# Attention's v loaded whole, its raw weight pieces in two buffers, w_in by wider pieces: one kernel of attention, experts and a second layer

## The chip, the cores and the metric

One NeuronCore of a Trainium2 chip runs the whole program. The metric is the device time of one execution in microseconds (us); less is better. A profiled execution gives the span (from the first to the last instruction) and the trace from which the rows below are taken.

## The reference

Three layers follow each other on 4608 tokens of width 512. First an attention within chunks of 64 tokens, for 8 heads of 64 features:

```python
scores = scale * np.matmul(q_c, k_c.transpose(0, 1, 2, 4, 3))
scores = scores - np.max(scores, axis=-1, keepdims=True)
attn = np.exp(scores)
attn = attn / (np.sum(attn, axis=-1, keepdims=True) + 1e-09)
out = np.matmul(attn, v_c)
```

Then a layer of 8 experts (512 to 1024 to 512 with a relu between), of which each token goes to the one with the highest gate logit and is weighted by its softmax. Last a second layer over all tokens, with float64 weights `w_in` (512 x 2048) and `w_out` (2048 x 512):

```python
h = x @ w_in
g = np.maximum(h, 0.0) + alpha * np.minimum(h, 0.0)
return (g @ w_out).astype(np.float32)
```

## The kernel before, in words

The tokens are 36 tiles of 128. The attention works on one tile (two chunks) in a step; the order of all parts of a step, and how many steps back each of them works, is a table written by hand (`STEP`), walked by the loop at the end of `attention_and_routing`. A part's instructions go to their engines' queues in this order, and each queue runs in order. In a step TensorE computes the scores of the next tile (`scores`, L651), turns the exponents (`transpose_p`, L671), multiplies them by v (`weigh`, L688, into the accumulator `av`), and turns the result (`transpose_x`, L714); every second step it computes gate logits (`logits`, L734) and turns them (`turn_logits`, L750). DVE takes the maxima (`peak`, L656), divides by the sums of the rows (`normalise`, L700 to L703) and adds the logits (`sum_logits`, L756). ACT does the exponentials (L664) and copies (L676, L721). Later steps also rank the tokens of each expert and build a table of places (`rank` L799, `spot_low` L840, `spot_high` L847, `place` L857).

q, k and v come in pairs of tiles, all on SP's queue: q whole, on 128 partitions; k and v by halves. Two heads lie on the partitions. For k and v each half of the partitions is written into columns of its own and the rest is zero (`kbd`, `vbd`, zeroed once by memsets), so a product over all 128 partitions serves two heads at once. Two such operands exist of each, used in turns; a load waits on SP until the operand's last use is over, and what stands behind it on SP waits too.

Beside the attention the kernel converts the float64 weights of the second layer (`Float64Weights`). There are 32 pieces: piece 2f is 128 columns of `w_in`, piece 2f + 1 is 128 rows of `w_out`. A piece is loaded raw (512 KB), and passes the stages `bits` (DVE, L227 and L228), `round` (ACT L238, POOL L239), `square` (ACT L245), `mask` (DVE, L253) and `finish` (ACT L266, POOL L267). In the attention a piece takes three steps (table `CONV`): `bits` and `round` in the first, `square` and `mask` in the second, `finish` in the third. `bits` reads and `mask` last reads the raw buffer. With one buffer the next load is issued after `mask`:

```python
conv.use(cpool, 1)
```

Twelve pieces are converted in the attention. The other twenty follow in the first of the second layer's 12 groups, where two raw buffers exist. Before step f of that group, `experts_and_ffn` makes sure that enough pieces are finished; its tables hold enough conversions that this loop adds none.

After the attention a tail, again in an order by hand (`TAIL`), ends the routing while the first blocks of one expert are computed. Then the second layer and the experts run side by side, also by tables, mostly bound to TensorE.

Of the kernel before, what the change touches and what calls it, by code (L numbers as in the profile page):

```python
# [20 lines left out]
N = 4608            # tokens  # L21
D = 512             # model width
H = 8               # heads
E = 8               # experts
F = 1024            # expert width
F2 = 2048           # second layer's width
NF = F2 // P
NT = N // P         # token tiles
NPAIR = NT // 2
KMAX = NT           # blocks of 128 tokens of one expert: at most this many  # L30
NCODE = E * KMAX
MID = float(N // 2)
HP = H // 2         # pairs of heads
ROW = D + 4         # a row of the expert layer's output, and its token's row
GT = 3              # token tiles in a group of the second layer
NG = NT // GT
GW = GT * P
ROUTE = (12, 8, 4, 4, 4, 4)  # token tiles that are ranked together
EARLY = 3           # after these, some expert surely has GT full blocks: its first GT blocks come first
assert sum(ROUTE) == NT and ROUTE[-1] == 4 and sum(ROUTE[:EARLY]) * P >= E * GW  # L40
ENDS = {sum(ROUTE[:i + 1]): n for i, n in enumerate(ROUTE)}
TE = sum(ROUTE[:EARLY])  # rows of x_tok, g_tok and out: by place in the tile, then tile, first TE tiles, then the others
V65 = 64 + 1         # columns of a head of v: its features and a one
RAWS = 2            # pieces of expert weights being loaded

# The other tokens: slots of up to two blocks of one expert, first the pairs of full blocks, then pairs with a second
# block that is not full, then single blocks. With NP slots for pairs, at most E single blocks are left.
# [4 lines left out]
FP, FS = F // P, F // PAIR  # steps of a pair's slot, of a single block's  # L52

# A step of the attention: its parts in order, each for the tile so many steps back.
# [12 lines left out]
# A step of the second layer, and with it one of the experts: in the first group, with single blocks, and the others.  # L67
# [32 lines left out]
FRONT = 30           # steps of the experts in the first group  # L100
# [24 lines left out]
# Before the first step of the second layer.  # L125
# [7 lines left out]
HOLD = 5            # steps of the second layer that are finished tile by tile  # L133

def surely_done(n):
    """Tokens in the first n slots, and before them: at least this many."""
# [18 lines left out]
class Float64Weights:  # L155
    """The second layer's float64 weights, rounded to float32 from their words, in two parts of 12 bits each.

    Piece 2 * f is columns f * 128 to f * 128 + 127 of w_in, piece 2 * f + 1 is rows f * 128 to f * 128 + 127 of w_out.
    """

    PIECES = 2 * NF
    # The square of the smallest high word (read as float32) whose number is a normal float32.
# [10 lines left out]
    def hold(self, pool):  # L173
        """Room for half of the parts."""
        f = NF // 2
        self.parts.append([
            pool.tile([P, 4, f * P] if i < 2 else [P, f, D], F32R, name=f"w{i}_{len(self.parts)}") for i in range(4)
        ])
# [4 lines left out]

    def w_out_part(self, part, f):
        return self.parts[f // (NF // 2)][2 + part][:, f % (NF // 2), :]

    def use(self, pool, bufs):
        """The pool for the pieces from here on."""
        assert self.piece is None and self.masked is None
        self.pool, self.bufs, self.ahead = pool, bufs, 1  # L190
        self.load()

    def leave(self):
        """The pieces loaded are the last of this pool."""
        self.ahead = 0

    def load(self):
        i, f = self.loaded, self.loaded // 2
# [4 lines left out]
        if i % 2 == 0:  # L203
            src = self.w_in.rearrange("(c p) f -> p c f", p=P)[:, :, f * 2 * P:(f + 1) * 2 * P]
            self.nc.sync.dma_start(raw.rearrange("p (c f) -> p c f", c=4), src)
        else:
            self.nc.sync.dma_start(raw, self.w_out[f * P:(f + 1) * P, :])
        self.raws[i] = raw

    def tick(self):  # L210
        """The next stage of a piece."""
# [6 lines left out]
    def bits(self):  # L218
        """The next piece: sign, exponent (its bias 127 for 1023) and the mantissa's bits in the high word."""
# [13 lines left out]
    def round(self):  # L233
        """The low word, rounded to 2^29."""
# [12 lines left out]
    def mask(self):  # L247
        """Zero for what is too small for a normal float32."""
# [7 lines left out]
    def finish(self):  # L256
        if self.masked is None:
            return
        nc, i, f, wf = self.nc, self.finished, self.finished // 2, self.masked
        self.finished, self.masked = i + 1, None  # L260
        if i % 2 == 0:
            hi, lo = self.w_in_part(0, f), self.w_in_part(1, f)
            wf = wf.rearrange("p (c f) -> p c f", c=4)
        else:
            hi, lo = self.w_out_part(0, f), self.w_out_part(1, f)
# [4 lines left out]
class Group:  # L270
    """Two layers over a few token tiles: activations by feature, then by token, every operand in two parts."""
# [11 lines left out]
    def take(self, rows, i, bank):  # L283
        """Token tile i of the group: its columns to partitions."""
# [29 lines left out]
    def up(self, key, wh, wl):  # L314
        """128 hidden features of all tokens."""
# [13 lines left out]
    def up_by_token(self, key, wh, wl):  # L329
        """The first tile's tokens, as many hidden features as the group is wide."""  # L330
# [27 lines left out]
    def down(self, acc, key, wh, wl, first, last, tiles=None):  # L358
        """Of some tiles: the last ones are the last that need this key."""
# [24 lines left out]
class Stream:  # L384
    """An expert's weights in pieces, in the order of their use: 256 columns of w1, then 256 rows of w2; each in two
    parts of 12 bits."""
# [8 lines left out]
    def add(self, index):  # L395
        """Another slot: where its expert's number is."""
        self.experts.append(index)
# [47 lines left out]
    def release(self, n):  # L445
        """Piece n has been used."""
# [20 lines left out]
class Gather:  # L467
    """The rows of a slot's tokens, their weights, and where they are."""
# [77 lines left out]
class Shared:  # L546
    """What the two parts of the kernel share."""


def attention_and_routing(ctx, tc, s_, qh, kh, vh, w_gate):  # L550
# [15 lines left out]
    # Operands with two heads on the partitions, each head's in its own columns, zeros elsewhere.  # L566
    kbd = [two.tile([P, 2, HP, 2 * P], F32, name=f"kbd{i}", bufs=1) for i in range(2)]
    vbd = [two.tile([P, 2, HP, 4, V65], F32, name=f"vbd{i}", bufs=1) for i in range(2)]
    for i in range(2):
# [3 lines left out]
        eng.memset(vbd[i][0:64, 1], 0.0)  # L573
        eng.memset(vbd[i][64:128, 0], 0.0)
# [6 lines left out]
    q_t = {}  # L581

    def load_halves(src, dst, j):
        for h2 in range(2):
            half = slice(h2 * 64, h2 * 64 + 64)
            d = dst[j % 2][half, h2]
            pat = "p a b -> p (a b)" if len(d.shape) == 3 else "p a b c -> p (a b c)"
            nc.sync.dma_start(d.rearrange(pat), src[j, half, :])
# [8 lines left out]
    def load_v(j):  # L597
        if j < NPAIR:
            load_halves(vh, vbd, j)
# [9 lines left out]
    # Constants.  # L609
# [72 lines left out]
    def weigh(t):  # L682
        a, vt = pt.pop(t), vbd[(t // 2) % 2]
        av = ps_av.tile([P, 2, 512], F32, tag="av", name="av")
        for hp in range(HP):
            for c in range(2):
                o = (hp % 2) * 2 * V65
                nc.tensor.matmul(  # L688
                    av[c * 64:c * 64 + 64, hp // 2, o:o + 2 * V65],
                    a[:, hp, c * 64:c * 64 + 64],  # L690
                    vt[:, :, hp, (t % 2) * 2 + c, :],
# [4 lines left out]
    def normalise(t):  # L696
# [7 lines left out]
            x.rearrange("p (a b d) -> p a b d", a=2, d=64), av[:, :, :, 0:64],  # L704
# [22 lines left out]
    def logits(t):  # L727
        """By pair of heads, each pair's on partitions of its own."""
# [33 lines left out]
    def choose(t0, n):  # L762
# [12 lines left out]
        # The gate's weight of the chosen expert: exp(0) over the sum.  # L775
# [608 lines left out]
```

## Time and profile before

| | |
|---|---|
| device time, three runs | 1571.5, 1567.76, 1571.31 us; median 1571.31 |
| span of the profiled execution | 1565.5 us, 24290 instructions |
| busy in it | PE 1492.6, DVE 841.7, ACT 662.9, POOL 454.1 us |
| DMA | 201.17 MB in 123508 packets |
| attention | first scores at 7.4 us, last at 163.0 us |
| second layer and experts | from about 236 us on |

The profiled execution's own time is not among the three runs; its span is the measure that belongs to the rows, and it lies 5.8 us below their median. PE is TensorE's matmuls, PEld its weight loads, SPq the issue of DMAs on SyncE's queue. In a row of instructions stand the start in us from the span's start, the duration, engine, line, operation, what is written from what, shapes and count, and in brackets how long the engine had stood idle and what ended that. A float32 product appears as two records.

### The profile page before, as it was taken

To read this page: it belongs to the slowest core of one execution; us is meant where nothing else is said; L and a number is where in the kernel's file an instruction comes from. 1 tells how busy PE (TensorE), PEld (TensorE's weight loads), DVE (VectorE), ACT (ScalarE), POOL (GpSimd) and SP (SyncE) were. 2 spreads that over 40 slices of the span, in tenths; PEclk is the share of its full clock that TensorE was granted. 3 is DMA by queue.
4 is the path that set the end of the run, shared out by engine and by line. 5 is a ranking of instruction groups with operands and counts; after the bars stand their busy time and mean duration, and the time that the engine had idled before them with its cause. 6 is when DMAs were issued, how large, how long until landed. Compare 5 with 4: busy or idle time off the path is not lost.

```text
span 1565.5 us, 24290 instructions
## 1 busy us (share of the span) xinstructions
PE 1492.6 (95%) x9160; PEld 1326.1 (85%) x9160; DVE 841.7 (54%) x1487; ACT 662.9 (42%) x1365; POOL 454.1 (29%) x430
## 2 busy tenths in 40 slices
PE   6888788899999999999999999999999999999998
PEld 5666577788899999999999999999998998998887
DVE  4678877777544444544444444445445555555443
ACT  5876536555433333433333334323324444444211
POOL 2235535666322221120321312203113223231100
PEclk9999899999999999999999999999999999999999
DMA  9998535555333223322422333323224544444000
GB/s 241 288 264 251 167 103 167 175 188 182 108 115 95 101 89 115 98 85 88 128 84 93 108 108 108 95 86 117 82 95 135 165 152 148 142 154 149 28 21 21
DMA packets 123508, 201.17 MB, mean 129 GB/s; under 512 B 12992, under 2 KB 72384, under 8 KB 123392
## 3 DMA queue, kind: packets, MB, share of 16 engines
q1 hardware_dynamic: 112496, 168.32, 35.6%
q0 software_dynamic: 10896, 31.31, 5.8%
q8 instruction: 72, 1.18, 0.3%
q14 instruction: 44, 0.36, 0.1%
HBM read 170.13 MB, written 29.46 MB: 127 GB/s over the span
## 4 chain that ended last, share of the span: by engine, by line
PE 76%; DVE 8%; DMA 6%; POOL 4%; issue 4%; ACT 2%; SPq 0%; POOLq 0%; ACTq 0%; DVEq 0%
PE fh L324 8%; PE fh L326 8%; PE fh L325 8%; PE fo L369 8%; PE fo L370 8%; PE fo L371 8%; PE mh L326 3%; PE mh L325 3%; PE mh L324 3%; PE mo L369 3%; DMA raw<-in_w_in 3%; PE mo L371 3%; PE mo L370 3%; DVE word L253 2%; PE tr L288 2%
## 5 line engine op out<-in xcount | busy, mean ns | idle before, releaser
L435 DVE TENSOR_TENSOR wlo<-raw,whi 128x1024 fp32r<-128x1024 f32 x146 | 183.8, 1264 | 171.2 <-ACT whi L427 170.4
L324 PE MATMUL fh<-fxh,w 128*128 128x384 f32 x760 | 257.0, 338 | 5.1 <-DVE fact L1195 4.3
L427 ACT CAST whi<-raw 128x1024 fp32r<-128x1024 f32 x200 | 208.8, 1049 | 122.5 <-PE mo L371 50.7
L326 PE MATMUL fh<-fxh,w 128*128 128x384 f32 x760 | 256.4, 337 | 0.0
L325 PE MATMUL fh<-fxl,w 128*128 128x384 f32 x760 | 255.6, 336 | 0.5 <-DVE fxl L296 0.5
L435 POOL TENSOR_TENSOR wlo<-raw,whi 128x1024 fp32r<-128x1024 f32 x54 | 129.7, 2402 | 430.2 <-ACT whi L427 418.9
L1194 DVE TENSOR_SCALAR fact<-fh,alpha 128x384 f32<-128x384 f32 x190 | 116.9, 615 | 232.1 <-PE fh L326 231.8
L369 PE MATMUL fo<-w,fgh 128*128 128x512 f32 x567 | 225.0, 397 | 0.0
L370 PE MATMUL fo<-w,fgh 128*128 128x512 f32 x567 | 222.7, 393 | 0.0
L371 PE MATMUL fo<-w,fgl 128*128 128x512 f32 x567 | 221.8, 391 | 0.0
L1127 ACT ACTIVATE mact<-mh 128x256 f32<-128x256 f32 x160 | 61.2, 382 | 287.1 <-PE mh L326 284.7
L305 ACT CAST fgh<-fact 128x384 fp32r<-128x384 f32 x197 | 100.8, 512 | 179.7 <-DVE fact L1195 179.3
L324 PEld LDWEIGHTS fh<-fxh,w 128*128 128x128 f32 x760 | 143.2, 188 | 14.7 <-DVE fact L1195 6.0
L325 PEld LDWEIGHTS fh<-fxl,w 128*128 128x128 f32 x760 | 143.1, 188 | 8.4 <-DVE fxl L296 0.8
L324 PE MATMUL mh<-mxh,whi 128*128 128x256 f32 x512 | 144.0, 281 | 1.3 <-ACT mact L1127 1.3
L326 PE MATMUL mh<-mxh,wlo 128*128 128x256 f32 x512 | 144.5, 282 | 0.0
L325 PE MATMUL mh<-mxl,whi 128*128 128x256 f32 x512 | 144.3, 282 | 0.0
L326 PEld LDWEIGHTS fh<-fxh,w 128*128 128x128 f32 x760 | 142.7, 188 | 0.0
L311 DVE TENSOR_TENSOR fgl<-fact,fgh 128x384 fp32r<-128x384 f32 x197 | 115.1, 584 | 35.7 <-ACT fgh L305 35.7
L311 DVE TENSOR_TENSOR mgl<-mact,mgh 128x256 fp32r<-128x256 f32 x128 | 63.1, 493 | 119.5 <-ACT mgh L305 119.5
L371 PEld LDWEIGHTS fo<-w,fgl 128*128 128x128 f32 x567 | 106.5, 188 | 23.5
L369 PEld LDWEIGHTS fo<-w,fgh 128*128 128x128 f32 x567 | 107.0, 189 | 17.4
(235 smaller groups left out, 2738.5 us busy)
## 6 DMA issues: line engine op xcount, KB each, us to landing
raw<-in_w SPq DMA_DIRECT2D x200, 512.0 KB, 3.6
vbd<-in_vh SPq DMA_DIRECT2D x36, 260.0 KB, 5.6
qt<-in_qh SPq DMA_DIRECT2D x18, 512.0 KB, 7.7
kbd<-in_kh SPq DMA_DIRECT2D x36, 256.0 KB, 8.0
x_tok<-x SPq DMA_DIRECT2D x36, 256.0 KB, 6.6
x<-y_sorted SPq DMA_DIRECT2D x33, 258.0 KB, 4.1
raw<-in_w_in SPq DMA_DIRECT2D x16, 512.0 KB, 5.9
raw<-in_w_out SPq DMA_DIRECT2D x16, 512.0 KB, 4.7
```

Of the source, the lines that this page charges most:

```text
L305: self.nc.scalar.copy(gh, self.g[key])
L311: self.nc.vector.tensor_sub(gl, t, gh.bitcast(F32))
L324: nc.tensor.matmul(b, wh[:, c, :], hi[:, c, :], start=(c == 0), stop=False)
L325: nc.tensor.matmul(b, wh[:, c, :], lo[:, c, :], start=False, stop=False)
L326: nc.tensor.matmul(b, wl[:, c, :], hi[:, c, :], start=False, stop=(c == 3))
L369: nc.tensor.matmul(o, gh[:, s], wh, start=first, stop=False)
L370: nc.tensor.matmul(o, gh[:, s], wl, start=False, stop=False)
L371: nc.tensor.matmul(o, gl[:, s], wh, start=False, stop=last)
L427: self.nc.scalar.copy(hi, raw)
L435: (engine or (self.nc.gpsimd if n % 4 == 3 else self.nc.vector)).tensor_sub(lo, raw, hi.bitcast(F32))
L1127: nc.scalar.activation(t, b, AF.Relu)
L1194: nc.vector.tensor_scalar(t, b, 0.0, s_.alpha[:, f:f + 1], op0=ALU.min, op1=ALU.mult)
```

## The change

Three things change together. v of a pair of tiles is loaded by one DMA over all 128 partitions into a tile without zeros (two buffers), and `weigh` multiplies each head by itself: 64 partitions times 64 columns of the array, 65 columns of v, with each of the two heads in a bank of its own; `normalise` puts the heads back in order. The attention's conversions get a second raw buffer, so that the load of the next piece is issued by `bits`. Of every four pieces, two are now 256 columns of `w_in` by half of the rows, and two are 128 rows of `w_out`; `needed` says how many pieces step f asks for.

```diff
+    def w_in_piece(self, part, i):
+        f, c = i // 4 * 2, i % 4 * 2
+        k = f % (NF // 2)
+        return self.parts[f // (NF // 2)][part][:, c:c + 2, k * P:(k + 2) * P]
+    def w_out_tile(i):
+        return i // 4 * 2 + i % 4 - 2
+    def needed(f):
+        return f // 2 * 4 + f % 2 + 3
...
-        if i % 2 == 0:
-            src = self.w_in.rearrange("(c p) f -> p c f", p=P)[:, :, f * 2 * P:(f + 1) * 2 * P]
-            self.nc.sync.dma_start(raw.rearrange("p (c f) -> p c f", c=4), src)
+        if i % 4 < 2:
+            f, c = i // 4 * 2, i % 4 * 2
+            src = self.w_in.rearrange("(c p) f -> p c f", p=P)[:, c:c + 2, f * 2 * P:(f + 2) * 2 * P]
+            self.nc.sync.dma_start(raw.rearrange("p (c f) -> p c f", c=2), src)
...
-    vbd = [two.tile([P, 2, HP, 4, V65], F32, name=f"vbd{i}", bufs=1) for i in range(2)]
-        eng.memset(vbd[i][0:64, 1], 0.0)
-        eng.memset(vbd[i][64:128, 0], 0.0)
...
     def load_v(j):
         if j < NPAIR:
-            load_halves(vh, vbd, j)
+            v_t[j] = two.tile([P, HP, 4, V65], F32, tag="vt", name="vt")
+            nc.sync.dma_start(v_t[j].rearrange("p a b c -> p (a b c)"), vh[j])
...
-            for c in range(2):
-                o = (hp % 2) * 2 * V65
+            for h2, c in ((0, 0), (1, 1), (0, 1), (1, 0)):
+                h, q = slice(h2 * 64, h2 * 64 + 64), slice(c * 64, c * 64 + 64)
                 nc.tensor.matmul(
-                    av[c * 64:c * 64 + 64, hp // 2, o:o + 2 * V65],
-                    a[:, hp, c * 64:c * 64 + 64],
-                    vt[:, :, hp, (t % 2) * 2 + c, :],
+                    av[q, h2, hp * V65:(hp + 1) * V65], a[h, hp, q], vt[h, hp, (t % 2) * 2 + c, :],
                     start=True, stop=True,
                 )
...
-            x.rearrange("p (a b d) -> p a b d", a=2, d=64), av[:, :, :, 0:64],
+            x.rearrange("p (b a d) -> p a b d", a=2, d=64), av[:, :, :, 0:64],
...
-    conv.use(cpool, 1)
+    conv.use(cpool, 2)
...
-            while g == 0 and conv.finished < min(2 * f + 2, conv.PIECES):
+            while g == 0 and conv.finished < conv.needed(f):
```

How the instructions stand on two queues (the line numbers of the changed kernel are its own: L600 is k's load, L605 q's, L612 v's, L220 and L223 the raw pieces', L723 the store of x). SP at the start of the attention, from the load of the second pair's q on; before:

```order
L593 DMA qt<-in_qh 128x1024
L588 DMA kbd_115<-in_kh 64x1024 x2
L588 DMA vbd_117<-in_vh 64x1040 x2
L205 DMA raw_171<-in_w_in 128x4x256
L593 DMA qt<-in_qh 128x1024
L588 DMA kbd_114<-in_kh 64x1024 x2
L207 DMA raw_250<-in_w_out 128x1024
L593 DMA qt<-in_qh 128x1024
L588 DMA kbd_115<-in_kh 64x1024 x2
L588 DMA vbd_116<-in_vh 64x1040 x2
L711 DMA x_tok<-x 128x512
```

The same place with the change:

```order
L605 DMA qt<-in_qh 128x1024
L600 DMA kbd_115<-in_kh 64x1024 x2
L612 DMA vt<-in_vh 128x1040
L220 DMA raw_165<-in_w_in 128x2x512
L220 DMA raw_203<-in_w_in 128x2x512
L605 DMA qt<-in_qh 128x1024
L600 DMA kbd_114<-in_kh 64x1024 x2
L605 DMA qt<-in_qh 128x1024
L600 DMA kbd_115<-in_kh 64x1024 x2
L223 DMA raw_326<-in_w_out 128x1024
L612 DMA vt<-in_vh 128x1040
L723 DMA x_tok<-x 128x512
```

v is one load instead of two, and the second raw piece is issued right behind the first, ahead of the third pair's q and k; the third piece follows where before the second was just through.

TensorE in the first steps (`s` are the scores, `bp` the turned exponents, `av` the products with v); before:

```order
L651 MATMUL s<-kbd_115,qt 64x128 x8
L688 MATMUL av<-vbd_116,pt 64x130 x8
L671 MATMUL bp<-ident,pr 128x128 x4
L651 MATMUL s<-kbd_114,qt 64x128 x8
L688 MATMUL av<-vbd_116,pt 64x130 x8
```

The same place with the change:

```order
L664 MATMUL s<-kbd_115,qt 64x128 x8
L702 MATMUL av<-vt,pt 64x65 x16
L684 MATMUL bp<-ident,pr 128x128 x4
L664 MATMUL s<-kbd_114,qt 64x128 x8
L702 MATMUL av<-vt,pt 64x65 x16
```

The groups keep their places; each `av` group has twice the products with half of the columns. SP at the end of the attention, where the last v is loaded, with the change:

```order
L800 DMA g_tok<-g_all 128x4
L723 DMA x_tok<-x 128x512
L220 DMA raw_2658<-in_w_in 128x2x512
L612 DMA vt<-in_vh 128x1040
L723 DMA x_tok<-x 128x512
```

The raw load there is the thirteenth piece's. Before, no raw load stood between this store and v's load, and the thirteenth piece was the first of the second layer's.

## Rows read from the trace of the kernel before

**Rows 1.** The page, its first two lines: span, and busy time by engine.
```profile
span 1565.5 us, 24290 instructions
PE 1492.6 (95%) x9160; PEld 1326.1 (85%) x9160; DVE 841.7 (54%) x1487; ACT 662.9 (42%) x1365; POOL 454.1 (29%) x430
```

**Rows 2.** Busy time by stretches: stretch and length, engines in the order of the first line.
```profile
core 0: us, PE busy (x) PEld busy (x) DVE busy (x) ACT busy (x) POOL busy (x), PEclk, DMA share, GB/s
20.50:45.20 24.70, 20.89 (x244) 16.58 (x243) 14.47 (x37) 20.55 (x74) 5.14 (x4) 0.95 0.94 256
45.20:69.71 24.51, 22.37 (x271) 17.00 (x270) 14.46 (x40) 19.62 (x66) 5.14 (x4) 0.98 1.01 293
69.71:98.74 29.03, 24.81 (x284) 18.89 (x284) 20.12 (x58) 20.86 (x71) 7.16 (x6) 0.88 0.94 266
98.74:125.92 27.18, 24.50 (x281) 18.27 (x280) 20.00 (x55) 21.88 (x75) 15.11 (x14) 0.98 0.95 273
125.92:155.10 29.18, 26.09 (x296) 19.76 (x295) 25.02 (x85) 20.04 (x66) 15.33 (x15) 0.96 0.91 254
155.10:175.00 19.90, 16.31 (x196) 12.47 (x196) 17.79 (x61) 15.30 (x49) 10.02 (x10) 1.00 0.81 237
```

**Rows 3.** Waits of DVE, 18 to 180 us: total us, times, longest.
```profile
DVE word L227 <- DMA raw<-in_w_in: 21.5, 6, 5.7
DVE word L227 <- DMA raw<-in_w_out: 1.2, 2, 0.8
```

**Rows 4.** Timeline of SP, DVE and PE about one wait.
```profile
31.24 0.38 SPq L205 DMA_DIRECT2D raw<-in_w_in  x1
40.20 0.43 DVE L227 TENSOR_SCALAR word<-raw 128x512 int32<-128x512 int32 x1 [4.89 <-DMA raw<-in_w_in]
42.54 1.68 PE L688 MATMUL av<-vbd,pt 128*64 128x130 f32 x16 [3.21 <-DVE lg_all L756]
```

**Rows 5.** Timeline of PE: scores of tiles 10 and 12.
```profile
49.75 1.09 PE L651 MATMUL s<-kbd,qt 128*64 128x128 f32 x16
...
57.01 1.09 PE L651 MATMUL s<-kbd,qt 128*64 128x128 f32 x16
```

**Rows 6.** Raw landings: w_in before 200 us; w_in, then w_out, 240 to 400.
```profile
DMA to landing us min/median/max: 6.9/7.9/8.9
...
DMA to landing us min/median/max: 3.7/4.6/6.0
...
DMA to landing us min/median/max: 4.2/4.7/6.7
```

**Rows 7.** Waits of DVE, 236 to 405 us: the only one for a raw piece.
```profile
DVE word L227 <- DMA raw<-in_w_out: 1.4, 1, 1.4
```

**Rows 8.** DMA, 0 to 9 us in 40 slots: GB/s.
```profile
GB/s 0 0 0 0 0 0 0 36 218 73 127 382 419 382 437 346 291 309 291 273 182 237 255 274 239 203 240 296 203 241 185 240 296 206 102 294 212 114 170 311
```

**Rows 9.** PE: one av and one gate group, records of each (min/median/max), one ranking.
```profile
62.42 1.11 PE L688 MATMUL av<-vbd,pt 128*64 128x130 f32 x16
...
L688 PE MATMUL av<-vbd,pt x576: 272/273/478, 22.3 to 176.9; 128*64 128x130 f32 x192
...
61.85 0.64 PE L734 MATMUL lgb<-xt,wg 128*32 128x256 f32 x8
...
L734 PE MATMUL lgb<-xt,wg x144: 379/403/634, 34.8 to 190.5; 128*32 128x256 f32 x144
...
87.47 0.50 PE L799 MATMUL rkb<-oh,ones 128*128 128x96 bf16 x12
```

**Rows 10.** Timeline at the start: SP, DVE, PE.
```profile
8.93 0.59 SPq L205 DMA_DIRECT2D raw<-in_w_in  x1
17.72 0.43 DVE L227 TENSOR_SCALAR word<-raw 128x512 int32<-128x512 int32 x1 [5.71 <-DMA raw<-in_w_in]
18.86 1.71 PE L671 MATMUL bp<-ident,pr 128*128 128x128 f32 x4 [2.45 <-ACT pr L664]
```

**Rows 11.** Timeline of DVE and PE in the tail.
```profile
182.94 3.25 DVE L769 TENSOR_TENSOR ra<-ra,wdown 128x32 f32<-128x32 f32 x1
187.39 1.12 PE L288 MATMUL bf<-ident,x 128*128 128x128 f32 x4 [6.61 <-DVE xt L721]
```

More of the change, by code (lines that the diff above doesn't have):

```diff
@@ L182, in w_in_part @@
         return self.parts[f // (NF // 2)][part][:, :, k * P:(k + 1) * P]
+    def w_in_piece(self, part, i):
+        f, c = i // 4 * 2, i % 4 * 2
+        k = f % (NF // 2)
+        return self.parts[f // (NF // 2)][part][:, c:c + 2, k * P:(k + 2) * P]
+    @staticmethod
+    def w_out_tile(i):
+        return i // 4 * 2 + i % 4 - 2
+    @staticmethod
+    def needed(f):
+        return f // 2 * 4 + f % 2 + 3
     def w_out_part(self, part, f):
@@ L197, in load @@
     def load(self):
-        i, f = self.loaded, self.loaded // 2
+        i = self.loaded
         if i >= min(self.started + self.ahead, self.PIECES):
@@ L202, in load @@
         raw = self.pool.tile([P, 2 * D], I32, tag="raw64", name="raw64", bufs=self.bufs)
-        if i % 2 == 0:
-            src = self.w_in.rearrange("(c p) f -> p c f", p=P)[:, :, f * 2 * P:(f + 1) * 2 * P]
-            self.nc.sync.dma_start(raw.rearrange("p (c f) -> p c f", c=4), src)
+        if i % 4 < 2:
+            f, c = i // 4 * 2, i % 4 * 2
+            src = self.w_in.rearrange("(c p) f -> p c f", p=P)[:, c:c + 2, f * 2 * P:(f + 2) * 2 * P]
+            self.nc.sync.dma_start(raw.rearrange("p (c f) -> p c f", c=2), src)
         else:
+            f = self.w_out_tile(i)
             self.nc.sync.dma_start(raw, self.w_out[f * P:(f + 1) * P, :])
@@ L258, in finish @@
             return
-        nc, i, f, wf = self.nc, self.finished, self.finished // 2, self.masked
+        nc, i, wf = self.nc, self.finished, self.masked
         self.finished, self.masked = i + 1, None
-        if i % 2 == 0:
-            hi, lo = self.w_in_part(0, f), self.w_in_part(1, f)
-            wf = wf.rearrange("p (c f) -> p c f", c=4)
+        if i % 4 < 2:
+            hi, lo = self.w_in_piece(0, i), self.w_in_piece(1, i)
+            wf = wf.rearrange("p (c f) -> p c f", c=2)
         else:
-            hi, lo = self.w_out_part(0, f), self.w_out_part(1, f)
+            hi, lo = (self.w_out_part(part, self.w_out_tile(i)) for part in range(2))
         nc.scalar.copy(hi, wf)
@@ L546 @@
 class Shared:
+    pass
 def attention_and_routing(ctx, tc, s_, qh, kh, vh, w_gate):
@@ L579, in by_tile @@
         return a[TE * P:].rearrange("(p t) d -> p t d", t=NT - TE)[:, t0 - TE:t0 - TE + n, :]
-    q_t = {}
+    q_t, v_t = {}, {}
     def load_halves(src, dst, j):
@@ L586, in load_halves @@
             d = dst[j % 2][half, h2]
-            pat = "p a b -> p (a b)" if len(d.shape) == 3 else "p a b c -> p (a b c)"
-            nc.sync.dma_start(d.rearrange(pat), src[j, half, :])
+            nc.sync.dma_start(d.rearrange("p a b -> p (a b)"), src[j, half, :])
     def load_qk(j):
@@ L682, in weigh @@
     def weigh(t):
-        a, vt = pt.pop(t), vbd[(t // 2) % 2]
+        a, vt = pt.pop(t), v_t[t // 2]
         av = ps_av.tile([P, 2, 512], F32, tag="av", name="av")
         for hp in range(HP):
-            for c in range(2):
-                o = (hp % 2) * 2 * V65
+            for h2, c in ((0, 0), (1, 1), (0, 1), (1, 0)):
+                h, q = slice(h2 * 64, h2 * 64 + 64), slice(c * 64, c * 64 + 64)
                 nc.tensor.matmul(
-                    av[c * 64:c * 64 + 64, hp // 2, o:o + 2 * V65],
-                    a[:, hp, c * 64:c * 64 + 64],
-                    vt[:, :, hp, (t % 2) * 2 + c, :],
+                    av[q, h2, hp * V65:(hp + 1) * V65], a[h, hp, q], vt[h, hp, (t % 2) * 2 + c, :],
                     start=True, stop=True,
```

## The prediction

> **What bounds the kernel now.** First the page: TensorE is busy 1492.6 of 1565.5 us [rows 1], so a gain must come from a stretch in which it waits. Cut by stretches, the attention is such a place. I cut it at the starts of the scores of tiles 3, 9, 15, 21, 27 and 33, six steps to a stretch [rows 2]: PE is busy 20.9 to 26.1 us of 24.5 to 29.2, and in the same stretches the 16 DMA engines are busy 0.91 to 1.01 of the time. ACT has about 20.6 us of work in each, DVE 14.5 at first and 25.0 in the fifth. So four resources stand close together, and whatever is taken away, the next one is near.
>
> Who waits for what: between 18 and 180 us DVE stands 21.5 us, six times, for a piece of `w_in` and only 1.2 us for `w_out` [rows 3]. One of these waits in order [rows 4]: the load is issued at 31.24 us, when `mask` has read the only buffer; DVE comes to `bits` 4.89 us before it has landed and stands until 40.20; its queue holds everything else of that step, `normalise` and `sum_logits` among it, and so TensorE stands 3.21 us until 42.54. Without such a wait TensorE has no gap: tile 10's scores start at 49.75 and tile 12's at 57.01 [rows 5], 7.26 us for two steps, 21.8 for six. Five stretches of six steps took 134.6 us together [rows 2], 25.6 more than five times 21.8.
>
> **The change, part by part.** The sum is made against this execution, whose span is 1565.5 us; the median of the runs is 5.8 us above that, and I take the difference of the sum off the median.
>
> *Second raw buffer.* Nothing is added on an engine: the same conversions in the same order on ACT, DVE and POOL. On SP a load moves from behind `mask` to behind the `bits` of the piece before, so it has three steps, 10.9 us by rows 5, to land instead of less than two. Landing in the attention took 6.9 to 8.9 us for `w_in` [rows 6], so the wait for it should go. Piece 1 now stands on SP ahead of tiles 4 and 5's q and k; it needs no wait, and q and k have over a step in hand. No load is new on the queue but the thirteenth, which moves out of the start of the second layer; after 236 us DVE waited for a raw piece once, 1.4 us [rows 7], so this is worth 0 to 1.4 and I take 0.
>
> *v loaded whole.* 18 loads of 520 KB replace 36 of 260 KB on half of the partitions. What halves cost is seen at the start, where the queue is otherwise empty [rows 8] (a slot is 0.225 us): the first q, over all partitions, moves at 346 to 437 GB/s, mean 393 over slots 12 to 16; in the 19 slots after it, the halves of k and v, it is 102 to 309, mean 240. 520 KB are 0.532 MB: 2.22 us at 240, 1.35 at 393, so 0.87 us of the DMA engines per pair of tiles and 2.6 per six steps. The stretch with the fullest DMA took 24.5 us at a share of 1.01 [rows 2]; less 2.6, six steps need 21.9 us of the DMA engines. The Trainium skill, page "SBUF — State Buffer", section "Door 1: The DMA port swizzle", says that partitions 0 to 63 reach no more ports than 0 to 31, eight of sixteen, and gives half the rate; by its 218 and 436 GB/s the saving would be 1.2 us per pair, an estimate, and six steps would need 20.9. The trace has the halves at 240, not 218, and the rows' value stands in the sum.
>
> *Pieces of w_in by 256 columns.* Half as many packets, each twice as long. In the second layer, where there is room, a `w_in` piece lands in 3.7 to 6.0 us and a `w_out` piece, whose rows are four times as long, in 4.2 to 6.7 [rows 6]: no price for the short packets, so I take 0. Step 6 of the second layer needs 15 finished pieces instead of 14; the conversions run ahead of that, and the order of ACT, DVE and POOL is as before: 0.
>
> *Products on quarters.* Eight products of 130 columns (16 records) become 16 of 65 (32 records). A group took 1.11 us with 16 records of 273 ns [rows 9], two parts of the array at a time. Two ends: the gate's products use four parts, and eight records of 403 ns fit into 0.64 us [rows 9], so if quarters run side by side too, a part has eight records of half the length, some 0.43 us less, a group of 0.68. If they do not, 32 records at the present pace of 0.056 us (the difference of group and record, 0.84, over 15) add 0.89, a group of 2.00. I think the first the more likely, since rows show parts of one array running side by side, but count none of it in the sum: with 21.9 us DMA stands level with TensorE's 21.8 anyway. `normalise` writes x in steps instead of in a row; its other side was already in pieces; taken 0. Four memsets of v's zeros go, two of them on POOL ahead of the gate weights' memset, for which SP waits.
>
> **The sum.** Start: DVE waits 5.71 us for the first piece, issued at 8.93, and TensorE stands 2.45 at the end of it [rows 10]; v is on the way before it twice, 2 x 0.87, and SP gets there earlier: 2.0 us. Stretches one and two go to 22.0 (21.9 and 21.8, whichever is last): 2.7 and 2.5. Three holds the first ranking of 12 tiles and ran at a granted clock of 0.88; with 24.8 us PE busy, part of it slow, I take 23.5: 5.5. Four has the table's products on PE, 24.5 busy, now 24.0: 3.2. Five is DVE's, 25.0 busy plus small waits, 26.5: 2.7. From 155 to 175 us DVE is busy 17.8 of 19.9: 0.9. Together 19.5. Against it 1.5 for new short waits of TensorE for k, since four resources are now within a tenth of each other. The rest of the program moves up as it is. **18 us: 1571.3 - 18 = 1553.3.** What is late next: k by halves on the DMA queue in the first half of the attention, DVE in the second.
>
> **Rivals.**
> *The quarters count* (0.20). If DMA falls under 21 us for six steps, 0.43 us per tile come through in stretches one to four, down to ACT's 20.6: 1.3 + 1.3 + 2 + 2, so 6.5 more, 1547. For it: the gate's rows. The Trainium skill speaks against it, page "TensorEngine Tiling (Array Packing)", section "Instruction Overhead": each product carries some 60 cycles, and one should not tile along a dimension that is already small. A row near it is the ranking's [rows 9], twelve products of 8 to 96 columns in 0.50 us, about 0.03 apiece; at that pace 32 records take about what 16 take now, and the time stays at the forecast.
> *DMA stays the bound* (0.16). If whole v gains nothing in the traffic, six steps stay at 24.5 and the waits for `w_in` become waits for k: savings 1 + 0.2 + 0 + 4 + 1.7 + 2.2 + 0.6, about 10, 1562. For it: shares of 0.91 to 1.01 [rows 2]. Against it: TensorE ran 7.26 us pairs with no wait for k.
> *It does not do what it says* (0.07): the landing stretches with the deeper queue and the wait only moves; within 0.3%, 1569.
> *Slower* (0.07). The quarters run one after the other, 2.00 us a group. TensorE then needs 21.8 + 5.3 = 27.1 for six steps, with the ranking and the table 28.5, 29 and 31; with 22 for the end, 164.7 against 154.5 now, less 2 at the start: 8 slower, 1579. It decides from about 0.6 us more per group on, where (154.5 + 2 - 137) / 33 is used up; that is, from a group of 1.7.
>
> **How the numbers follow.** Forecast 0.50, and its own range is 1548 to 1559: the tail can shift by some 3 us either way, since there DVE instructions of 128x32 took 3.25 us beside POOL's work and TensorE waited 6.61 for it [rows 11], and such meetings move. The range takes in the first two rivals, 1543 to 1566. A measurement here can tell some 0.3%, 4.7 us, from no change. Faster by more: 0.50 + 0.20 + 0.16 = 0.86; within: 0.07; slower: 0.07.
>
> **What would show it.** Right: DVE's wait for `w_in` between 18 and 180 us under 4 us in place of 21.5; tile 33's scores at about 137 us in place of 155.1; `av` groups at 0.7 to 1.1 us; packets as many bytes at 300 GB/s or more in the first stretches. Wrong: TensorE waiting over 6 us for k (DMA the bound), `av` groups over 1.7 us (slower), or the second layer beginning later by more than the attention ends earlier.

## The result, and the profile after

The changed kernel takes 1549.0 us (median of four runs, 1545.0 to 1552.8) against 1569.5 us before on the same chip; the ratio is 0.9891, 95% interval [0.9868, 0.9914]. A second measurement (e7, below) gave 0.9869 [0.9845, 0.9893]. Forecast were 18 us less; 1.1 to 1.3% of 1569.5 are 17 to 21. (The two medians by themselves lie 20.5 us apart, a quotient of 0.9869; below, the recorded ratios with their intervals are used.) The profiled execution spans 1543.2 us, 22.3 less than that of before; from here on times in a profile are compared with times in a profile, and measured ratios with ratios.

The page's head, to be laid beside [rows 1]:

```profile
span 1543.2 us, 25420 instructions
PE 1475.8 (96%) x9736; PEld 1313.8 (85%) x9736; DVE 834.1 (54%) x1485; ACT 660.8 (43%) x1365; POOL 451.9 (29%) x428
```

TensorE has 576 more instructions and is busy for 16.8 us less. Where the time went is seen in the same stretches as in [rows 2], cut again at the scores of tiles 3, 9, 15, 21, 27 and 33 (columns as there):

```profile
core 0: us, PE busy (x) PEld busy (x) DVE busy (x) ACT busy (x) POOL busy (x), PEclk, DMA share, GB/s
17.88:37.73 19.85, 18.34 (x340) 14.32 (x339) 14.12 (x37) 18.89 (x67) 5.12 (x4) 0.91 0.96 296
37.73:61.16 23.43, 20.13 (x367) 14.79 (x366) 14.76 (x40) 20.12 (x70) 5.13 (x4) 1.00 1.03 317
61.16:85.77 24.61, 20.32 (x380) 15.21 (x379) 19.24 (x56) 20.91 (x72) 7.14 (x6) 1.00 1.02 320
85.77:108.16 22.39, 21.09 (x378) 16.06 (x377) 18.73 (x56) 20.09 (x69) 14.73 (x14) 1.00 0.99 315
108.16:134.65 26.49, 22.79 (x393) 17.08 (x392) 24.98 (x83) 21.02 (x72) 15.93 (x15) 1.00 0.96 300
```

Five stretches take 116.8 us in place of 134.6. The DMA engines are now busy at 0.96 to 1.03 in all of them and move 296 to 320 GB/s instead of 254 to 293. TensorE's busy time fell by 2.2 to 4.5 us a stretch. In e7, a second profile of the same kernel, the five stretches take 20.8, 22.6, 25.5, 22.0 and 26.5 us at shares of 0.85, 1.04, 1.03, 1.03 and 0.99: a single stretch differs by up to 1 us between executions, so a reading of one stretch to a tenth says little.

The waits of DVE from 18 to 180 us, all that are listed (beside [rows 3]):

```profile
DVE x L715 <- DMA x_tok<-x: 12.0, 10, 2.7
DVE den L712 <- PE av L702: 7.1, 11, 1.8
DVE den L712 <- remote: 2.7, 1, 2.7
DVE mx L669 <- PE s L664: 2.5, 4, 1.5
DVE lo L852 <- PE tb L869: 2.1, 1, 2.1
DVE fxl L312 <- ACT fxh L308: 0.9, 1, 0.9
DVE word L269 <- ACT raw L261: 0.4, 1, 0.4
```

No wait for a raw piece is left. In its place stands one for the store of an earlier tile's x: 12.0 us, ten times, where before it was 1.5. TensorE from 10 to 170 us has a new wait too, for k, 0.7 us before the change:

```profile
PE s L664 <- DMA kbd<-in_kh: 6.6, 7, 2.1
PE av L702 <- issue: 4.9, 2, 3.3
```

In the timeline, the first conversion at the start, one group of products with v, the scores of the last tile, and the first product of the tail (before: 17.72 us [rows 10], 1.11 us long [rows 9], 162.96 and 179.73 us):

```profile
15.25 0.43 DVE L243 TENSOR_SCALAR word<-raw 128x512 int32<-128x512 int32 x1 [3.71 <-DMA raw<-in_w_in]
56.48 0.70 PE L702 MATMUL av<-vt,pt 64*64 64x65 f32 x32
142.47 0.77 PE L664 MATMUL s<-kbd,qt 128*64 128x128 f32 x10
150.18 0.70 PE L702 MATMUL av<-vt,pt 64*64 64x65 f32 x32 [1.68 <-issue]
155.16 1.45 PE L702 MATMUL av<-vt,pt 64*64 64x65 f32 x32 [3.27 <-issue]
162.04 0.66 PE L304 MATMUL bf<-ident,x 128*128 128x128 f32 x4
```

So the attention gains 20.5 us up to the last scores. Then 2.8 are lost up to the tail (the two waits in which the profile names no releaser), 3.5 come back in the tail, where TensorE's wait for `xt` is 2.0 us instead of 6.6 [rows 11], and 2.1 are lost on the way to the experts' first product, at 226.16 in place of 245.24. From there to the end this execution is 3.2 us shorter than that of before; the profiles of the twelve experiments, with the old and the new pieces of `w_in`, lie between 1317.2 and 1318.9 us there and before alone at 1320.3, so I count these 3 us as that execution's, not as the change's.

### The profile page after: what moved, and what is told of

It is laid out like the page before. It is cut to its first block, busy times and chain, and to the rows that moved or that the text cites. A ratio compares the mean times of both kernels' runs of the same rounds, so it can differ in the third digit from the quotient of the medians.

```text
span 1543.2 us, 25420 instructions
## 1 busy us (share of the span) xinstructions
PE 1475.8 (96%) x9736; PEld 1313.8 (85%) x9736; DVE 834.1 (54%) x1485; ACT 660.8 (43%) x1365; POOL 451.9 (29%) x428
## 4 chain that ended last, share of the span: by engine, by line
PE 77%; DVE 8%; DMA 6%; POOL 3%; issue 3%; ACT 1%; SPq 0%; POOLq 0%; another core or an unknown queue 0%; ACTq 0%; DVEq 0%
PE fh L340 8%; PE fh L342 8%; PE fh L341 8%; PE fo L385 8%; PE fo L386 8%; PE fo L387 8%; PE mh L342 3%; PE mh L341 3%; PE mh L340 3%; PE mo L385 3%; PE mo L387 3%; PE mo L386 3%; DMA kbd<-in_kh 2%; DVE word L269 2%; PE tr L304 2%
## 5 line engine op out<-in xcount | busy, mean ns | idle before, releaser
L387 PEld LDWEIGHTS fo<-w,fgl 128*128 128x128 f32 x567 | 106.5, 188 | 23.4
```

The source lines that it names most:

```text
L387: nc.tensor.matmul(o, gl[:, s], wh, start=False, stop=last)
```

## The experiments

The theories: **the buffer** (one raw buffer made DVE wait, DVE's queue held TensorE; the second buffer is the gain) against **the traffic** (the DMA engines were the bound; v whole is the gain, and the wait for `w_in` was only where it showed). Beside them stood the question whether the quarters' shorter groups counted. Measured, with the ratio to the kernel before on the same chip, what the ratio makes of 1569.5 us, and from each profile the start of tile 35's scores and TensorE's wait for k between 10 and 170 us:

| | ratio, 95% interval | us | tile 35 | wait for k |
|---|---|---|---|---|
| before | | | 163.0 | 0.7 |
| whole change | 0.9891 [0.9868, 0.9914] | -17.1 | 142.5 | 6.6 |
| e7, the same again | 0.9869 [0.9845, 0.9893] | -20.6 | 143.8 | 5.0 |
| e1, buffer alone | 0.9931 [0.9909, 0.9954] | -10.8 | 153.9 | 5.3 |
| e2, v alone | 0.9932 [0.9907, 0.9957] | -10.7 | 156.2 | 3.9 |
| e3, v and w_in, one buffer | 0.9933 [0.9911, 0.9956] | -10.5 | 155.2 | 4.8 |
| e4, buffer and w_in, v as before | 0.9913 [0.9878, 0.9947] | -13.7 | 149.8 | 4.3 |
| e5, whole, v loaded by halves | 0.9931 [0.9908, 0.9955] | -10.8 | 153.5 | 12.3 |
| e6, whole, quarters in turn | 0.9915 [0.9892, 0.9938] | -13.3 | 155.3 | none |
| e8, whole, k whole too | 1.0049 [1.0030, 1.0067] | +7.7 | 174.3 | 0.8 |
| e9, whole, most of k not loaded | 0.9812 [0.9792, 0.9832] | -29.5 | 135.4 | none |
| e10, whole, w_in narrow | 0.9872 [0.9849, 0.9894] | -20.1 | 145.4 | 9.4 |
| e11, whole, four x | 0.9893 [0.9872, 0.9914] | -16.8 | 141.1 | 7.0 |
| e12, whole, x stored in pairs | 0.9877 [0.9850, 0.9904] | -19.3 | 146.0 | 8.9 |

**e1, the buffer alone.** The kernel before with

```diff
-    conv.use(cpool, 1)
+    conv.use(cpool, 2)
```

> The kernel before with the second raw buffer as its only edit; v still by halves on products of 130 columns, w_in by 128 columns. Two theories, against 1569.5 us before and 1549.0 with the whole change. The buffer (mine): DVE's wait for w_in, 21.5 us in the kernel before, falls under 4 us, and the halves of v and the short packets cost the DMA engines some 1.1 and 0.8 us per six steps (packet times per MB of both traces), which now show as TensorE's waits for k: 1549 + 5 x 1.9 + 2.6 at the start = about 1561, at most 1564. The traffic: the DMA engines were the bound and the wait for w_in only where it showed; then a wait for k takes its place and the time is 1567 or more.

Measured: 10.8 us less, 1558.7 on the scale of 1569.5, as the buffer theory said and a little better. Of DVE's waits for a raw piece only the one at the start is left, and TensorE now waits for k:

```profile
DVE word L227 <- DMA raw<-in_w_in: 5.7, 1, 5.7
PE s L651 <- DMA kbd<-in_kh: 5.3, 3, 2.3
```

(The row of before with 21.5 us counts the wait at the start too, which ends at 17.72 with an instruction that reaches past 18; without it five waits of together 15.8 stand there.) The traffic theory in its strict form, 1567 or more, falls.

**e2, v alone.** The kernel before with the new `load_v`, `weigh` and `normalise`, as in the diff of the change.

> The kernel before with v loaded whole and multiplied by quarters as its only edit; one raw buffer, w_in by 128 columns. The buffer (mine): the start gains 2.6 us, the landing of the raw pieces gets some 0.5 us shorter, but the six waits for w_in stay at 15 us or more together: about 1562, not under 1558. The traffic: most of the gain is here, 1556 or less. In both cases an av group takes 0.70 us wherever TensorE is at its upper clock level, as in the kernel with the whole change.

Measured: 10.7 us less, as much as the buffer. That is better than I had expected, yet not the 13.5 that the traffic theory wanted; the interval, 6.7 to 14.6 us less, takes in both figures, so the time alone doesn't decide between them. The wait for `w_in` shrank, from the 15.8 us just named, instead of staying:

```profile
DVE word L227 <- DMA raw<-in_w_in: 11.9, 5, 4.5
DVE word L227 <- DMA raw<-in_w_out: 1.6, 3, 0.7
```

**e3, one buffer.** The changed kernel with `conv.use(cpool, 1)`.

> The changed kernel with one raw buffer in the attention. The buffer (mine): the waits for w_in come back, 10 to 16 us together, and with them most of the loss: 1558 to 1564. The traffic: with v whole and w_in by 256 columns the waits stay small, under 6 us, and the time within 4 us of the changed kernel, under 1553.

Measured: 10.5 us less than before, so the second buffer carries some 7 to 10 us of the whole. The waits are back:

```profile
DVE word L243 <- DMA raw<-in_w_out: 9.3, 6, 3.7
DVE word L243 <- DMA raw<-in_w_in: 6.2, 3, 3.2
```

They add to 15.5 us, as the buffer theory said. e2 and e3 differ only in the pieces of `w_in`, and not in the time.

**e4, v as before.** The changed kernel with the loads, zeros and products of v of the kernel before.

> The changed kernel with v as before: two loads of 64 partitions into an operand with zeros, eight products of 130 columns. The buffer (mine): the start loses 2.6 us and each of five stretches of six steps 1.1 us of the DMA engines, so about 1557 (1554 to 1560), with TensorE's waits for k grown from 6.6 to 12 us. The traffic: 1563 or more. If TensorE's own time counted too (groups of 1.11 us in place of 0.70), each stretch would lose up to 2.4 us, 1563 as well, but then TensorE would show no waits for k.

Measured: 13.7 us less than before, in the expected range (1556 on the scale of 1569.5). Its interval, 8.3 to 19.1 us less, overlaps those of the whole change, so by the time alone the loss isn't clear of noise. The wait for k did not grow, it is 4.3 us; and where nothing waits, two steps take 7.26 us as in [rows 5] (scores at 48.62 and 55.88). In the fourth stretch TensorE is busy without a pause, where the changed kernel takes 22.4 (22.0 in e7; columns as in the result):

```profile
91.60:115.15 23.55, 23.54 (x281) 17.87 (x280) 19.34 (x54) 20.37 (x69) 14.95 (x14) 1.00 1.02 307
```

With the old groups TensorE's own pace held part of the time, which my theory had left out.

**e5, v by halves, quarters kept.**

```diff
-            nc.sync.dma_start(v_t[j].rearrange("p a b c -> p (a b c)"), vh[j])
+            for half in (slice(0, 64), slice(64, 128)):
+                nc.sync.dma_start(v_t[j][half].rearrange("p a b c -> p (a b c)"), vh[j, half, :])
```

> The changed kernel, quarters kept, but each v loaded by two DMAs of 64 partitions, as before. What the older form of v costs (tile 35's scores at 149.8 us in e4 against 142.5) is thereby parted into transfer and products. Transfer (mine): the halves alone bring most of it back, tile 35's scores at 147 to 150 us, TensorE's waits for k grow, 1550 to 1556. Products: the quarters' 0.4 us per group were what came through; then tile 35's scores stay under 145 us and the time within 2 us of the changed kernel.

Measured: tile 35's scores at 153.5, later than I had expected, and 10.8 us less than before in place of 17 to 21 (1558.7 on the scale of 1569.5, past the 1556 that I had named). The same row as in the changed kernel:

```profile
PE s L665 <- DMA kbd<-in_kh: 12.3, 9, 2.4
```

Halves of v alone double the wait for k. Since the quarters are still there, their shorter groups bought nothing that the time shows here: TensorE came to the scores sooner and waited longer. That e5 is later than e4 in the profile (153.5 against 149.8) isn't explained; in the ratio the two don't differ.

**e6, quarters in turn.**

```diff
-        for hp in range(HP):
-            for h2, c in ((0, 0), (1, 1), (0, 1), (1, 0)):
+        for h2, c in ((0, 0), (1, 1), (0, 1), (1, 0)):
+            for hp in range(HP):
```

> The changed kernel with the 16 products of a group in another order: four of one quarter behind each other, then four of the next. If a product can only run beside others of other quarters, a group takes 1.6 to 2.0 us in place of 0.70, the rival 'slower' of the prediction in the flesh: TensorE needs some 26 us for six steps, tile 35's scores come at 165 to 180, 1565 to 1580. If the order does not matter (products of one quarter follow each other as closely), the group stays under 0.9 us and the time at 1549.

Measured: a group takes 1.54 us, 2.2 times as long as in the changed order, and TensorE has no gap. Scores of tiles 9 and 11, and a group between them:

```profile
43.23 1.09 PE L664 MATMUL s<-kbd,qt 128*64 128x128 f32 x16
45.41 1.54 PE L702 MATMUL av<-vt,pt 64*64 64x65 f32 x32
51.35 0.88 PE L664 MATMUL s<-kbd,qt 128*64 128x128 f32 x12
```

Two steps take 8.12 us: 7.26 less two groups of 1.11 and plus two of 1.54. Six take 24.4, where the changed kernel takes 23.4 to 24.6 in the second and third stretch though TensorE could do them in 19.3 (7.26 less 0.82, three times). So 0.84 us more in each of 36 groups, 30 us, came through with 12 in the attention and 4 to 7 in the end. I had expected 1565 to 1580; I had set the added work against a TensorE without slack, and it had some 4 us per stretch.

**e7, the changed kernel again.**

> The changed kernel unchanged, for a second profile. In the first, TensorE stood 1.68 and 3.27 us at 150 and 155 us for nothing that the profile names, and DVE 2.7 and ACT 3.3 for a releaser that it does not know, which no other kernel's profile shows. If that belongs to the kernel (the loads around the last v, or the code of 32 more instructions per tile), it is there again, about as long, and tile 35's scores to the first bf product take 19.6 us again; if it is chance, they take about 17.

Measured: chance. Those waits are not there, and tile 35's scores to the first `bf` product take 16.2 us. (Waits without a named releaser occur here too, at another place: 2.9 us in two waits before scores, 2.3 of them at 68 us.)

```profile
159.97 0.66 PE L304 MATMUL bf<-ident,x 128*128 128x128 f32 x4
```

In its tail TensorE then waits 6.6 us for `xt`, as in the kernel before, and the experts' first product is at 225.5 in place of 226.2. What one stretch of the tail gave, another took.

**e8, k whole.** k is loaded as v; `scores` is cut in two by head, and `peak` too:

```diff
-                nc.tensor.matmul(s[c * 64:c * 64 + 64, hp, :], qt[:, hp, cs], kt[:, :, hp, cs], start=True, stop=True)
+                nc.tensor.matmul(s[c * 64:c * 64 + 64, hp, h], qt[h, hp, cs], kt[h, hp, cs], start=True, stop=True)
...
+        half_scores(t, 0)
+        half_peak(t, 0)
```

> The changed kernel with k as v: one load of 512 KB over 128 partitions, no zeros and no memsets, the scores of each head by itself on 64x64 parts; the two heads of a pair share a bank, so the second head's products wait until DVE has taken the first one's maximum, which makes two maxima of 256 columns of one of 512. The traffic (mine: after the change the DMA engines bind, 0.96 to 1.03 of the five stretches): six steps need some 2 us less of them, TensorE's waits for k (6.6 us) go, and five stretches save 1 to 2 us each, with DVE's extra instruction against it in the fifth: tile 35's scores at 133 to 138 us and the time 1540 to 1546. If four resources stand level and TensorE or ACT binds instead: within 2 us of 1549, or slower, as TensorE then waits for DVE in each step.

Measured: a miss, 7.7 us slower than before. The DMA engines needed less for a MB (2.97 us in place of 3.17, packets of 20 to 140 us), and the wait for k fell to 0.8 us. But TensorE now waits 15 times for DVE, and DVE 42 times for TensorE (10 to 170 us):

```profile
PE s L653 <- DVE mx L657: 10.0, 15, 1.6
...
DVE mx L657 <- PE s L653: 40.4, 42, 2.6
```

By tile 24 the attention was 8 us behind the changed kernel (exponents turned at 111.1 against 103.2; 5 behind e7, 105.8). Then the granted clock fell, and stayed low for some 65 us (stretches of 12 us, columns as above):

```profile
92.00:104.00 12.00, 11.60 (x243) 8.76 (x241) 9.67 (x31) 10.72 (x37) 6.58 (x6) 1.00 0.88 294
104.00:116.00 12.00, 9.95 (x212) 7.51 (x211) 9.11 (x27) 9.15 (x29) 7.74 (x7) 1.00 0.92 319
116.00:128.00 12.00, 12.00 (x134) 9.11 (x133) 7.54 (x31) 6.52 (x24) 4.49 (x5) 0.50 0.67 221
...
164.00:176.00 12.00, 12.00 (x143) 8.97 (x145) 7.21 (x22) 6.11 (x19) 3.53 (x4) 0.50 0.39 105
176.00:188.00 12.00, 11.37 (x180) 8.55 (x175) 10.32 (x36) 8.01 (x20) 10.44 (x11) 0.80 0.66 235
```

Tile 35's scores came 31 to 32 us later than in the changed kernel, so most of that loss fell in the stretch of the low clock; 5 to 8 us of it stood before. As a test of the traffic it says little, since it put another chain in its place; e9 does that without one.

**e9, most of k not loaded.**

```diff
-            load_halves(kh, kbd, j)
+            if j < 2:
+                load_halves(kh, kbd, j)
```

> The changed kernel without the loads of k from the third pair on (16 of 18 pairs; the scores of all later tiles are taken with the first two pairs' k, so what it computes is not the attention). It takes 8.4 MB off the DMA queue and nothing off any engine. If the traffic binds the changed kernel (mine), six steps fall to what ACT and TensorE need, 20 to 21.5 us in the stretches that take 23.4, 24.6 and 22.4 now: tile 35's scores at 131 to 137 us in place of 142.5 and 143.8, the time 1536 to 1543. If the traffic does not bind: tile 35 not before 141, the time within 2 us of 1547.

Measured: 29.5 us less than before, 1540.0 on the scale of 1569.5, 9 to 12 less than the changed kernel; tile 35's scores 7 to 8 us earlier. Both are what the traffic theory said. The same five stretches:

```profile
19.73:38.12 18.39, 17.67 (x339) 13.79 (x339) 14.00 (x37) 18.39 (x67) 5.13 (x4) 0.95 0.77 252
38.12:57.92 19.80, 19.64 (x368) 14.62 (x367) 14.94 (x40) 19.80 (x70) 5.14 (x4) 1.00 0.90 300
57.92:79.75 21.83, 20.17 (x380) 15.19 (x379) 18.42 (x55) 20.67 (x72) 7.13 (x6) 1.00 0.83 271
79.75:100.77 21.02, 21.02 (x377) 16.03 (x377) 19.23 (x54) 20.03 (x69) 14.28 (x13) 1.00 0.88 279
100.77:127.58 26.81, 22.90 (x393) 17.01 (x392) 25.25 (x84) 21.30 (x72) 16.43 (x16) 1.00 0.68 219
```

With room on the queue the first two stretches end at ACT, busy 18.39 of 18.39 and 19.80 of 19.80, the fourth at TensorE, 21.02 of 21.02, and the fifth does not move: DVE is busy 25.25 of 26.81. So after the change the traffic binds stretches two to four (3.6, 2.8 and 1.4 us; 2.8, 3.6 and 1.0 against e7), with ACT and TensorE right behind it. For the first it isn't shown: e9 enters it later, at 19.73 in place of 17.88 (18.58 in e7), and leaves it at 38.12, where the changed kernel does so at 37.73 (39.40 in e7).

e9 takes off more than bytes: TensorE no longer waits for a landing of k at all, and k's loads no longer stand on SP's queue. That queue can hold them up in the changed kernel, for it stands before the loads of v until a buffer is free, with the next q and k behind them (18 to 165 us):

```profile
SPq L612 <- PE av L702: 35.7, 16, 4.9
```

Whether k would land in time with a third buffer for v, or ahead of v on the queue, at the same traffic, was not tried; shares of 1.02 and 1.03 in stretches two and three leave little room for it there.

**e10, w_in narrow.** The changed kernel with the pieces and `needed` of before, `2 * f + 2`.

> The changed kernel with w_in by 128 columns as before (packets of 1 KB). The prediction took the wider pieces at nothing; e2 and e3 agree with that, 0.9932 and 0.9933, but there a raw wait still bound. Traffic (mine): a narrow piece costs the DMA engines some 0.7 us more (4.3 against 2.9 us per MB), seven of them are loaded in the attention, and nearly all of it comes through: tile 35's scores at 146 to 149 us, 1550 to 1554. Nothing: within 2 us of 1547, tile 35 before 145.

Measured: 20.1 us less than before (1549.4 on the scale of 1569.5, between the two forecasts); no difference from the whole change can be seen. Tile 35's scores are 1.6 to 2.9 us later in this profile, in the expected direction and less than expected. My price was too high: in this kernel packets of 1 KB cost 3.4 us of the DMA engines per MB and those of 2 KB 2.9, so 0.3 us a piece, two in all.

**e11, four buffers for x.**

```diff
-        x = one.tile([P, D], F32, tag="x", name="x", bufs=3)
+        x = one.tile([P, D], F32, tag="x", name="x", bufs=4)
```

> The changed kernel with four buffers for x in place of three. In the changed kernel DVE waits 10.6 to 12.0 us, ten times, until an earlier tile's x is stored (1.5 us before the change): the stores now land late. If that wait is only where the full DMA queue shows (mine), its going leaves tile 35's scores at 140 to 144 us and the time within 2 us of 1547. If it is a wait of its own, handed on to TensorE over the products with v, tile 35 comes at 134 to 138 and the time is 1538 to 1543.

Measured: the wait for the store, 12.0 us, is gone from DVE's list, and the time stays, 0.9893. In its place DVE waits 14.4 us for the scores:

```profile
DVE mx L669 <- PE s L664: 14.4, 13, 2.9
```

The largest new wait of the changed kernel was a symptom.

**e12, x stored in pairs.** One store of 512 KB per two tiles, three buffers of two tiles.

> The changed kernel with x of two tiles in one buffer (three such buffers) and one store for both: packets of 4 KB in place of 2 KB, 18 stores in place of 36, each even tile's store a step later. By the packet times (94 ns for 2 KB, 161 for 4 KB) it takes 0.24 us of the DMA engines per pair, 0.7 per six steps. Traffic (mine): tile 35's scores 3 to 4 us earlier than in the changed kernel, with the wait for the store gone as in e11; 1541 to 1546. If the traffic does not bind, as e11.

Measured: no gain, 0.9877; tile 35's scores at 146.0, not 3 to 4 us earlier. Per MB the DMA engines needed 3.15 us in place of 3.17 (packets of 20 to 140 us), so the longer packets brought far less than the 0.7 us per six steps that I had reckoned, and TensorE's wait for k is 8.9 us. The price was at fault: it set a mean (94 ns for 2 KB) against a median (161 for 4 KB). Over all packets of the changed kernel from 20 to 140 us the medians are 84 and 162 ns and the means 93 and 224; by the medians the saving is 0.05 us per pair, by the means there is none. Whether k now stands behind the larger stores was not tried. None of the runs that compute the attention beats the changed kernel.

## Why the prediction was right

The forecast was 18 us less, with 1548 to 1559 for its own case; 1549.0 lies inside, and the two measured ratios, 17 and 21 us, lie on both sides of it. By its steps:

- **What bounds.** Four resources level, and the next one near: the traffic after the change, and in e9, without it, ACT, TensorE and DVE, each at the end of stretches of its own. e1 and e2 show what follows from that. Each part alone gives 11 us, and together they give 17 to 21; neither theory alone holds.
- **Second raw buffer.** The waits for `w_in` went to nothing, as said. "Worth 0 to 1.4, taken 0" for the thirteenth piece: DVE has no wait for a raw piece after 236 us any more, and the second layer shows no gain that other executions don't have.
- **v whole**, the term that was mis-sized. Length times share over the MB moved (windows of [rows 2] and of the result): the DMA engines needed 3.45 to 3.67 us per MB in the five stretches before and 3.14 to 3.25 after. In the data packets of 20 to 140 us e2, v whole alone, has 3.23 against 3.50, and the whole change 3.17 (3.21 in e7) against e4's 3.36 and against 3.50 in e5, where only v's load differs. So v whole is worth 0.19 to 0.33 us per MB, 1.4 to 2.4 per six steps of some 7.3 MB, where I had "0.87 us per pair, 2.6 per six steps" from the rates at the start: too high, by little if e5 is taken, which is the cleanest of the three. The second step that failed is the floor: "21.9" was taken from the second stretch, which already had the cheapest traffic (3.45), and for its old bytes. With the second buffer the raw pieces come sooner, 7.4 MB instead of 7.2 fell into it, and it took 23.4 in place of 22.0 (22.6 in e7). The Trainium skill, page "SBUF — State Buffer", section "Door 1: The DMA port swizzle", has half of the partitions at half of the rate in the limit, 218 against 436 GB/s, and at 196 against 328 GB/s as measured with 1 MiB. That halves cost more is what e5 shows, 3.50 us per MB again; but the rates at the start, 240 against 393, lie nearer to the second pair, and in the attention a packet of v took 239 ns on the median before and 161 after, 1.5 times as long, and on the mean, by which the engines' time adds up, 242 and 197, 1.2 times: not twice.
- **Quarters.** The first end was the price: 0.68 reckoned, 0.70 measured at a granted clock of 1.00. e6 shows that it hangs on the order, since in turn the same products take 1.54. The Trainium skill's rule of some 60 cycles per product, page "TensorEngine Tiling (Array Packing)", section "Instruction Overhead", spoke for no gain; by the group's row the 16 shorter products took 0.41 us less than the eight longer ones. I had counted none of it in the sum because DMA stood level. Where the traffic binds that was right, as e5 says. It was not in the fourth stretch, for which I had 24.0 of TensorE's work: e4, with the old groups, stays at 23.55 there with TensorE busy throughout, and the changed kernel takes 22.4. It also let the first stretch fall to 19.85 (20.8 in e7), below the 21.8 that I had as TensorE's floor (its steps have no gate products at first either).
- **The sum.** Start 2.6 (said: 2.0); stretches 4.9, 1.1, 4.4, 4.8, 2.7 (said: 2.7, 2.5, 5.5, 3.2, 2.7); the end of the attention, up to the last exponents turned at 150.8 in place of 172.3, 1.0 (said: 0.9). Together 21.5 against 19.5; the first and fourth stretch were forecast 2.2 and 1.6 too low, the second and third 1.4 and 1.1 too high, and the same signs hold in e7. That the total comes so close is in part luck, since these errors cancel. The allowance of 1.5 us for k is in these stretches. From there to the experts' first product the tail took 2.4 us back in this execution and 0.4 in e7's, within the 3 that I had left it.
- **The signs.** Tile 33's scores came at 134.65 (said: 137). The packets move 296 to 320 GB/s; the first stretch, with 296 (270 in e7), just misses the 300 that I had named for it. One sign of the rival "DMA stays the bound" came true as well: TensorE waits 6.6 us for k, over the 6 that I had named (5.0 in e7, under it). e9 speaks for its mechanism, but its price, 1562, left out that the traffic also got cheaper. The rival "the quarters count" had its 0.70 and not its bound: but for the first stretch, with few bytes (0.96 of 19.85 are 19.1 us), DMA did not fall under 21 us.
- **Slower.** e6 is that rival with 1.54 us in place of 2.00. It named 1.7 as the point from which it decides; at 1.54 the kernel is still faster than before, 0.9915.

## What to carry to other kernels

Where several resources stand level, write down for each stretch what each of them needs, and take the largest as the floor: a part of a change is then worth the way down to the next floor, and two parts on different floors add up. Take the price of a transfer from traffic like that in which it will run, not from an empty queue, and like against like, mean against mean. Profile the same kernel twice before you explain a single microsecond. A new wait of 12 us can be a symptom; give the waiting work another buffer and see whether the time moves.

## What the runs showed of the hardware

- Sixteen products on 64x64 quarters run side by side if neighbours in the queue lie on other quarters: 0.70 us a group, against 1.54 in turn. In turn, neighbours also write the same bank of the accumulator; quarter and bank were not parted.
- In e8 the granted clock was 0.50 (1.2 GHz) from 116 to some 181 us, while TensorE was busy 11.9 to 12.0 of each 12 us up to 176. Before it fell, TensorE had been idle 0.81 us at 105 and 1.24 at 114. In the first profile of the changed kernel idle times of 1.3 and 2.1 us passed at a granted clock of 1.00; in e7's, the clock fell beside idle times of 2.3 us at 68 and 1.1 at 115, and was back within 4 us. What kept it low in e8 was not found.
- In the same packet records, 4160 bytes of v took 161 ns on the median wherever v was loaded whole (nine kernels), and 205 to 239 where it came by halves. The means are less clear: 183 to 242 ns whole, 222 to 243 by halves. Over all data packets from 20 to 140 us, the kernels with v whole and k by halves needed 3.15 to 3.32 us of the DMA engines per MB, those with v by halves 3.36 to 3.50.
